# A new written-out order for an attention and feed-forward kernel on one core

## The chip, the cores and the metric

The kernel runs on one core of one Trainium2 chip. The metric is the device time of one execution in microseconds; the time of a version is the median of its runs. A core has five engines that the text names as the profile does: PE (TensorE, matrix products; PEld is its loading of weights), DVE (VectorE), ACT (ScalarE), POOL (GpSimd) and SP (SyncE, which here only issues transfers). Each engine works through its own list of instructions in order and waits on semaphores for the others.

## The reference

Inputs are q, k and v of shape (8, 8, 576, 64) (batch, heads, sequence, head width) and two weight matrices, all float32.

```python
def _attn_ref(q, k, v):                       # factor = 4
    q_d = q.reshape(B, H, Sd, factor, D).mean(axis=3)      # also k_d, v_d
    out_d = sm_attn(q_d, k_d, v_d)                         # attention on 144 pooled rows
    out_up = np.repeat(out_d, factor, axis=2)
    mask = np.abs(pos[:, None] - pos[None, :]) < factor    # a band of 7
    scores = np.where(mask, scale * np.matmul(q, k.transpose(0, 1, 3, 2)), -1e9)
    out_local = np.matmul(softmax(scores), v)
    return out_up + out_local

def _moe_ref(x, w_in, w_out):                 # x: (4608, 512), d_ff = 2048
    h = x @ w_in
    return (h - np.tanh(h)) @ w_out
```

The sum of the two attentions, laid out as 4608 tokens by 512, goes through the feed-forward part; its result is the output.

## The kernel before

The work is cut in two ways. Attention runs over 32 pairs of heads (8 batches of 4 pairs); the feed-forward part runs over 8 blocks, one for each batch, and block b needs all four pairs of batch b. The attention of later pairs is spread between the matrix products of earlier blocks.

**One pair** passes through these steps. SP loads k and q (tile `st`, line 341, 256 KB each), v (tile `vst`, line 365, two halves of 160 KB), and the last 64 rows of k and q of a batch (tile `sr`, line 353; for the first batch these two loads are issued by ACT). Casts to bf16 make `qr` (line 499), `rr` (line 489) and `vw` (line 425). For the first eight pairs PE turns `qr` over by identity matmuls (line 506; `rr` at line 529 into `rT`), and ACT or DVE copy the result to `kt` and `kq` (lines 511, 516, 533, 561, 566); for the later pairs SP issues a transposing transfer instead (line 550, line 544). Pooled q and k go to `qkd` (line 613 to 621 on PE for the first four pairs, lines 587 to 602 after). PE then makes the scores (lines 650, 660, 666), ACT the exponentials in three pieces into `E` (lines 671, 675, 679), DVE or POOL multiply by the band mask (line 706), PE sums pooled v for the first twelve pairs (line 456, from `vw`) and multiplies E with v (line 720). The result is divided (lines 736, 738), turned back by PE (line 763) or by SP (line 775), and joined into `xT` (line 756).

**One block** is 16 products with w_in (line 797, four matmuls of 128x512 each, issued as two halves), tanh on ACT into `u` (line 809), a subtraction on DVE into `gT` (line 812), and the product with w_out. The 64 left tokens of two batches share steps of their own (lines 824, 835, 837, 850). The first block multiplies with w_out plainly (line 878); the other seven do it in seven half-size products (line 1018) of sums and differences: `token_sums` (line 953) forms sums of quarters of gT, called S0 to S3, each choosing DVE or POOL, and `weight_sums` (line 927) those of w_out. ACT and POOL gather the results in `y`, and SP stores them (line 908).

**The order** is written out by hand. Each of 2,199 operations is recorded in a `Plan` together with what it reads and writes. Then `emit` goes through a string `TURNS`, in which two characters (base 62, digits, capitals, small letters) number one operation, and emits the operations in exactly that sequence. Thus the sequence fixes the order on each of the engines, SP's transfers among them, while the semaphores still hold back what isn't ready. Four more strings belong to it: `ENGINES` has a letter for each of the operations that may run on more than one engine (D for DVE, A for ACT, P for POOL); `BANKS` picks the PSUM banks; `FILL` puts matmuls on zeros ("filler", line 1227) ahead of an operation, a bank and a count behind its number; `BEHIND` lists pairs of operations of which the first waits for the second, for engines that share a port.

The operations that the next parts speak of are these. Number `10` is the cast of `rr` of batch 0, `11` and `12` are the casts of k and q of pair 0, `01` is a one-element copy on ACT (line 1150, tile `gate2`), recorded with a price of 1650 ns. `13` and `17` turn k and q of pair 0 over on PE. `3d` is the first matmul of the first block. `7V` is the issue of the second half of v of pair 11, `Ai` that of the transposing transfer of pair 13, `A9` the cast of v of pair 11, `BA` the sum of pooled v of pair 11 on PE (line 456). `Yb` is S0 of the last block.

SP has eight transfer semaphores: an issue waits until the transfer eight issues before it has landed.

Of the kernel before, what the change touches and what calls it, by code (L numbers as in the profile page):

```python
# [101 lines left out]
def kernel(  # L102
# [49 lines left out]
    ]  # L152

    TURNS = (
        "000E0F0I0J06020B0M0N030K0L0G0H0401050O0P0Q0R0D0A0W0X0U0V0e0f101d1e11131B0g0h1512141f1g16"
        "171H1P0Y0Z180C0S0T1I1J1Q0k0l1C1A1L1K19220c0d1M1D1R1S091N1T1u231w0i0j1U2R1O1V240a0b252T26"
        "2G2H1v1j1k08291x1y2Z1l1m27200y1W0o0p071z1E2S1n1o2y2a280m0n1F2U211X1G2b1Y2c2X1Z2V1p1q2d39"
        "0z2I2J2z2W1r5H2n2o1a2Y1s2p2q0q0r3A1b2A2g1c1h1i0s0t3B2B3N3O2e2C3D33303P3Q3C2O1t2t2u3E312P"
        "2D2M2N0u0v3F3G352v2E2f5I2w363H325J343I5L3J37385P5K2K2L5M2h5N2Q5S5O2i2j5U665Q3K5R2F682k5E"
        "3L5v3M2l5T632m5x5V3d5F5X3j643k5y3p5w3q3r5B3s5C613e5D5z3t3v3w5W3l603m3f623u3g3T3U655Y3n3x"  # L160
        "3h0w0x3o6e3y6g3i412r2s426U43475Z3z6c4D3R3S5a444849456T674E6b46694F4G5g5h6B4A406d5b4B4J4K"
        "5c3V3W4P5d4H4L4M4C4Q3X3Y4R5k5l4N6V4I6X5e5f6W4S4V6Y4b5m5n6Z6f4O4T4c4d6a4e2x4h4U7A4i4j4f4W"
        "6A4X4Y4g5s4Z4k4n4o4l4a4t4u5G4v5t4z4w3Z3a4m6C6h6j556i506D4p6E4x514q526Q4r4y7D536F4s567B7F"
        "576G586H7f3b3c6R8854597C7g895A728d7E5u6k7I71967G6l976m7H6y8e6z8E8j8F8k737J76779C7K6n7L7l"
        "74757m6o7M8K7N8p7O6I6J9D6p6u6v8qCG5i5j8L787rCB6K6L798v6M6N9f8w5o5p7s9g8x8Q5q5r9Z7xCD6w6x"
        "8R6s6tCF9h8S9i6q6r7yCC9j7X6O6PCE9I9k9J9a9m7b9l9b9c7z7cCH7Y7d7h9t9u9T6S7i7e9U7P7Q9O9V7Z9W"
        "9v9w9P7j9XAB7n7R7S7a9Q7oAA7k9Y9n70ACAD7t7p9oAd9p9d809zA09e81AG7q9qAbAcA79rA1A2827uAeAH9s"
        "847T7UA8857v83AgAI86Ah7w8AAKBDAiAj878BAJ8GCI8H8C8MATAUAEAF8I8NBaBb8V8DAMAm7V7W8W8J8OAo9x"
        "9y8Z8XALBGBH8fAq8a8PAnAN8Y8bBF8gAkAOApBEAP8l8hBMBIBJ8mAt8c8r8n8s8iA98yB0B1Ar8o8z8tEHEIDx"
        "BA908u92DtAVAW93BNBB91B2B3Al98ELEMCJ9EENEO9F94BOA5A6AsBP99BQBcBd959KBiEJEK9A9LEaAu9G9BDy"  # L170
        "BqBKBr9MDzE0E3AvCLAwBRBsBLCM9HE48T8UCRAZAaBtBTEb9NByBjE5E6CKCSE7EcEdBzEAC0BSC1BgBhE8AQCY"
        "C6BUCZE1C7C8CoARCpC9CABVEgE2BWCuA3A4CvB8B9ASAxF8D0EiEPEQAyBXEhAzEkAXAYD2BYEuEvD3BZDuCXIF"
        "D8EwExF7EjBkBlD9FeElDvF9FABmEeCaDEE9CbAfCgFTFUEmChEfIeIfEVBnCnFhFiEBCmBuBoBvEWEXEYDGFDBw"
        "IcIdDHECBCFEDMEDIgIhC2EnFfDNBxC3F2FFBpC4FGF3CNDSIGFBCOFgFHC5CTIJFjFkCUCPCcFnCdFIFoCVB4B5"
        "DTCQDUDFCeB6B7DZFKBeBfCfDaJxG3G4EoFCDfFVFWCiFZCWCjEEEFIKCqEpCkEqCrD1FlCwETEUCsCxClFpDwFJ"
        "FqD4ILIMCyD5IPFsDiD6CtIQDjF4F5DoFmCzErEsIHDpD7DAFrDBMUDqG1G2DIFaFRFSDCDJFtDOFXFYDKDPDDJS"
        "9R9SDVDQDLEGFbFcDWDbEyEzDRDXDcG7G8IwDkDYDdF0F1DlMVG9GJDeDmGOJREZGTDnERESGUFuGHFLIkIlINFv"
        "DrDsGZGIHhIIGcGhIOGaGiGnGbGuGsFMIvGzFNFdH0GAH5EtFwFOFPFxHmHAHrF6IRJ1FyFzHCITJ2HDISGtHIG5"
        "G6HNIVIxIyHwIqHSJ3IUHUK0K1J4FQHVHaG0J5JTJUIWJ7J6GDIuGEIXIrIiIjIYHfGFHTGKGBGCIzGLGGJEJFJ8"
        "GMJzJGJHHgGPJ0IZIaJXGQGNGVJ9GWJAGRJYImInGdJVGeMrMsGSJyGXJZIoIpHBGfGjGYK2K3GkJaHxGoK6GpGg"  # L180
        "GlMxMyI0GqGmGvIsItMZJWGwJMH1K7H2JOJPJbJNI5JmJnH3GrMYIAJkJlJdIBH4MWH6GxICH7IbK4K8GyH8HEMa"
        "MbKAHJMeK9HKHOJcJBJCHLHFH9HPMfHGJeHMMvMwJsHQHWJKJLHHKCHXNADgDhHbJfHYJtHRHcMtMuKRK5HiJgJI"
        "JJHjKBJuJvHnHZHdHoMzN0HkMgHeKJKKHsHpHlKLKMI1MhJqJrKuI2HtMcKDI3HqNBM4MiNGM5NCNDHuI4MAMkI6"
        "NHHvI7JhJiKZI8KSKaKEOCKFMdKwHyHzKbJDI9KcJQKxL2NEKvKGKHKhJwKiNFL3MjIDIEKjL9KkMlLAKpLPMmKq"
        "KrQmLQMnKsKtNhLVLWNTNUN5MBN6LbNIKILdNKNgLeNJJjNiNjLjLkNMNLKVO1O2LpKWNmN7N8NNL8NnKTKULrKX"
        "NOLqLBKPKQNPNkLCKNKONlLHKYODLIMGNoOELsOLNpOHOILxLOLyLNKdJoJpNqKeOMMoMpKlKfNbMJNrNsKmNVNW"
        "MKM3KnNcONOFOGQnKgMPO7OPKyOOKoQqNzO0KzMQLcNQNRL0L4MXL5L1LDN3N4L6OQLENdNeLJMRLFO8OaObLKMq"
        "ORL7NtN1N2LROJLGLSN9QrNuLXNvLTQwRJRKLfOSLLLUNwNxLYOKNSLMLgLlOTQsQtOULZLmQxLtLhLuLaRSOVOW"
        "LnQyOgLvLzLoM0RTNfRDRELiM6NyOeOfR0M7LwM1RBRCMCMDM8M2O3O4QoMLMEM9O9OAMMOqOXOYOZMFMNOvRURV"
        "QuP0MOQzP1OoOkOiOjP6OlNZNaOrQvOhOsNXNYR1P9RFRGOpOwOmSJSKOxOtPER9RAOnR2RYPFRlRmPKOuOyO5O6"  # L190
        "P2PPRWP3RHRIP7R3P4RnRoOzV1PARXV2PBP5RNPGR4PHRZR5PCPLPIPSS4PDR6R7PMPTPJPNRaRORPRQPUPYRzRb"
        "PdPVRtPZPORyPeRcPaPRP8S0S1PWPfS5PlRePbPmSURpRqPXOBPgV3RLRMS6PnPqOcOdSWS7PvPoSNSOPrRdRrRs"
        "PwPsMSMTQ3RuPxQ4PtR8PcQ5PyQ8PhQ9Q6SPQFQAV5RfSRSSSAQBQGSVQKS2RgSQSZSaQLQHSdQPQMQIQQRvRwRx"
        "PjRhPiSXSYPkS3PpQNQYV6SLSMPuQRSeQES8PQQZPzSfQaQ1QSQ0V7V8ShQ2QpQ7QbQCVUSjRiRjQJSgS9QOQTSH"
        "SISbRRSBQDVBMHMIQdV9QUSqSrT6VAVCSCTTSDQeScQXSiSESFQcQhTRQfQiT7TUVTT8SyQjTZSzTaVZQgVDT9VE"
        "VVVWVOTETSUbVFTFVHSsStUcTgQkQlTGTHThSkTMVGTwV4TPTQTxSlVPSmTNTOU2VaU3VQVRUhRkU8VIVXSnSoUA"
        "VJVYVuUBVKUGUHTfVvVbUMTiSGVfTjVoVcUOVpToUPVdSpVqVrSTTpVwTvT2T0T1VxT3SuSvVeUiVySwSxUUT4Vz"
        "UVVLVMTuVgT5UNVsTAW0UaTBTIVmVhViTJVnTVTKU9TWUnVjVkW1TXTLUqTCW9UoUpUrVtTbQVQWTDTcWAW2TkW3"
        "TdTlW7UwTYTmWBVNTnUxWDTqWCTeVSW4W5TyUyTrWFW8U4WETsTzUCTtVlU0WGU1U5UDW6WHWIUIUEUJU6UQUFWJ"
        "WKURUKU7UWUXULUzV0USUdUYUTUeUjUfUZWLUsUkUgUtWSUuWXUlWcUvWMUmWTWUWQWYWNWZWRWeWaWfWOWmWsWV"  # L200
        "WPWdWxWWWiX4WbWgX5WtWhWkWyXAWzWnWuWlX0XFWoXGWjWpXNWqX6XOXSX7XXWvXPWrWwXHXBXIXYXCXfXZXTXD"
        "XkXaXgXlXQXrXhXwY1X1XiX3XUX8XqXVY2X2XxX9XEXvXJXsXyYAYBXmXzXLXMXnXRXWY0XbYOY3YFXcXdXtY4Y5"
        "XKXeY6YPXjXuXoYbYCY9YGYdYHXpYEYJYDY7Y8YQYKYIYRYSYLYTYUYcYMYNYVYeYWYfYiYgYZYaZ2YXYYYjYkYw"
        "YxZ3YyZ4YhYzYlZ0YmYnZ5Z1YoYpZ7YqZ6YrZAZ8Z9YvYsZBYtYuZCZDZJZEZKZHZFZGZOZIZPZQZRZSZLZMZN"
    )
    ENGINES = (
        "DDDDADDAAPPDAAPADADADDDDPDDDDDADPDAPDPDDAADPADAAAPADAAADDDDDDAPAADAAPPPDDDPPADAAAPPPPDAA"
        "PPADADPPPPDDPPPPAAPPPPDAAAADPPDADDAADDDDAPPPDDPPDADAPPAAPPDDAAPPPAAPPDDPPADDDDDPPDAPPAAP"
        "PDPDDAPPAAPPDPPPADPAADPDDPPADPPAADDDDPPDDDDDPPPAPPAADPDPDPAPPAADDDPDDAPPAAPPDDPPAPPPAAPD"
        "PDPPADDDDDPPPAPPAADPDPDDAPPAAPPDPDPADPAADDDPPPAPPPAADDDPPDDDDDDPPPAPPAAPPDPPPAPPDAPPDDPD"  # L210
        "APPAAPDDDPPAPPPDAPDDDDPADDDDDPPPAPPAAPPDPDPPDPAAPPDPPPDPAAPPDPPPPPDPDPPPDADDDDD"
    )
    BANKS = (
        "0123456017206457012760113005223301301030203210230101210031212003321100112311002032011320"
        "3101102201310203110023210201301001012110130100113200123101231023110021010131032110321321"
        "0301120310120031021101001002101021130203110032103213120130120310120120012010112030110210"
        "1010030210301230102310230123674512365714327601524736120"
    )
    FILL = (
        "13715 1771 1L61 1w31 2431 1E01 1X72 3351 3H21 2h72"  # L220
    )
    BEHIND = (
        "1B11 2S0y 5H0z 2f3F 655W 7A6a AmAF AnAL BiAs EgCZ DFFo JSFt IvGb IrJ6 MYJN MfJc NBKu QmL"
        "A LqNn NcNr O8OQ RYOp V1P7 SUS5 R8Ru Q0PQ VPVG VuRk VpVo UNVz VlWE"
    )

    const = ctx.enter_context(tc.tile_pool(name="const", bufs=1))
# [60 lines left out]
    V, A, T, GP = nc.vector, nc.scalar, nc.tensor, nc.gpsimd  # L288
# [970 lines left out]
```

## Time and profile before

| | us |
|---|---|
| median of 3 runs | 316.26 |
| the runs | 314.4, 316.26, 320.43 |
| the profiled execution | 313.24 |
| its span, first to last instruction | 311.5 |

The profiled execution took 313.24 us, of which 311.5 us are its span. In the profile a window's line gives for each engine the busy time inside it with the number of instructions in brackets; a row of the timeline gives start, duration, engine, line, operation, tiles and shape, and in square brackets the idle time ahead of it with what ended it. A row of the timeline merges equal instructions that follow each other (x12). Matmuls are pipelined, so the duration of a merged row is a little longer than the time after which the next instruction can start; the chain of waits has that time itself.

### The profile page before, as it was taken

What the parts mean: (1) busy time and instruction counts of PE and PEld (TensorE: products, weight loads), DVE (VectorE), ACT (ScalarE), POOL (GpSimd) and SP (SyncE); (2) the same over time, 40 slices, a digit from 0 to 9 for tenths busy, and PEclk for the clock granted to TensorE, in tenths of its full rate; (3) what the DMA queues carried; (4) which work ended last, traced back from release to release, by engine and by line L of the source; (5) the groups of instructions that cost most, each with busy time, mean ns of one, the idle gap of its engine ahead of it and who ended that gap; (6) DMA issues with size and microseconds to landing.
All of it is one profiled execution on the core that took longest, in us unless ns stands there. A gap on an engine that the chain in (4) does not pass through costs nothing.

```text
span 311.5 us, 7779 instructions
## 1 busy us (share of the span) xinstructions
PE 299.8 (96%) x2982; PEld 198.2 (64%) x2982; DVE 248.4 (80%) x443; ACT 213.4 (68%) x378; POOL 167.4 (54%) x222
## 2 busy tenths in 40 slices
PE   6898999999899999999999999999999999999994
PEld 2575555554477655875587755656878655468783
DVE  3888875689988988998998978977995888564944
ACT  2888883289778887889886788888947675554110
POOL 5198869046684368338771379387624582911200
PEclk9999999999999999999999999999999999999999
DMA  6999999599998999989999999999999653000224
GB/s 208 266 269 239 219 240 186 137 258 260 222 227 238 281 182 257 258 154 233 262 288 262 242 230 177 242 260 252 150 184 196 151 171 93 3 0 2 100 71 136
DMA packets 120870, 60.81 MB, mean 195 GB/s; under 512 B 88832, under 2 KB 118528, under 8 KB 120832
## 3 DMA queue, kind: packets, MB, share of 16 engines
q1 hardware_dynamic: 115968, 55.53, 78.8%
q0 software_dynamic: 4224, 4.19, 8.1%
q10 hardware_dynamic: 640, 0.59, 0.6%
q8 instruction: 23, 0.38, 0.5%
q14 instruction: 15, 0.12, 0.1%
HBM read 44.04 MB, written 9.44 MB: 172 GB/s over the span
## 4 chain that ended last, share of the span: by engine, by line
PE 83%; DMA 7%; POOL 5%; SPq 1%; issue 1%; DVE 0%; ACTq 0%; POOLq 0%; DVEq 0%
PE ps L797 32%; PE ps L1018 28%; PE ps L720 5%; PE ps L850 4%; PE ps L878 4%; PE ps L824 4%; PE ps L650 2%; DMA vst<-in_v_dram 2%; DMA st<-in_q_dram 2%; DMA sr<-in_q_dram 2%; DMA kq<-qr 1%; POOL qr L499 1%; PE ps L666 1%; PE ps L763 1%; POOL qkd L592 1%
## 5 line engine op out<-in xcount | busy, mean ns | idle before, releaser
L797 PE MATMUL ps<-xT,w_in_sb 128*128 128x512 bf16 x512 | 121.4, 379 | 0.0
L812 DVE TENSOR_TENSOR gT<-ps,u 128x512 bf16<-128x512 f32 x128 | 84.9, 686 | 21.6 <-ACT u L809 21.0
L809 ACT ACTIVATE u<-ps 128x512 f32<-128x512 f32 x128 | 74.2, 599 | 29.8 <-PE ps L797 25.0
L797 PEld LDWEIGHTS <-w_in_sb 128*128 128x128 bf16 x512 | 47.7, 98 | 47.9
L1018 PEld LDWEIGHTS <-gT 128*128 128x128 bf16 x672 | 64.1, 98 | 15.6
L1018 PE MATMUL ps<-w_out_sb,gT 128*128 128x256 bf16 x336 | 43.4, 273 | 0.0
L1018 PE MATMUL ps<-Tw,gT 128*128 128x256 bf16 x336 | 42.3, 273 | 0.0
L499 POOL CAST qr<-st 128x512 bf16<-128x512 f32 x49 | 29.8, 616 | 16.4 <-DVE vw L1156 6.1
L671 ACT ACTIVATE E<-ps 128x912 bf16<-128x912 f32 x32 | 29.7, 930 | 9.1 <-PE ps L660 6.7
L738 DVE TENSOR_TENSOR ln<-ps,r 128x768 bf16<-128x768 f32 x32 | 30.6, 957 | 1.2 <-DVE r L736 0.2
L1089 POOL TENSOR_TENSOR y<-y,keep 128x512 f32<-128x512 f32 x12 | 15.2, 1273 | 26.1 <-ACT y L1039 15.0
L577 ACT COPY kt<-kq 128x576 bf16<-128x576 bf16 x23 | 27.2, 1187 | 1.7 <-DMA kq<-qr 1.5
L587 POOL TENSOR_TENSOR half<-kq 128x576 f32<-128x576 bf16 x16 | 20.4, 1276 | 13.4 <-ACT kq L572 5.5
L720 PEld LDWEIGHTS <-E 128*128 128x128 bf16 x576 | 21.4, 97 | 6.2 <-POOL E L706 1.5
L592 POOL TENSOR_TENSOR qkd<-half 128x288 bf16<-128x288 f32 x20 | 16.5, 823 | 13.0 <-DVE r L736 5.8
L679 ACT ACTIVATE E<-ps 128x576 bf16<-128x576 f32 x32 | 21.0, 655 | 1.8 <-PE ps L666 1.8
L706 DVE TENSOR_TENSOR E<-E,mask 128x1152 bf16<-128x1152 bf16 x26 | 20.2, 785 | 1.4 <-ACT E L671 0.7
L837 DVE TENSOR_TENSOR gL<-ps,u 128x512 bf16<-128x512 f32 x16 | 15.9, 1020 | 5.2 <-ACT u L835 5.2
L756 POOL TENSOR_TENSOR xT<-lT 128x336 bf16<-128x336 bf16 (+1 forms) x26 | 17.0, 678 | 5.2 <-DMA lT<-ln 3.1
L720 PE MATMUL ps<-vw,E 128*128 128x65 bf16 x320 | 19.0, 193 | 0.7 <-POOL E L706 0.7
L1039 ACT COPY y<-ps 128x512 f32<-128x512 f32 x19 | 11.1, 587 | 11.9 <-PE ps L1018 11.6
L425 ACT CAST vw<-vst 128x640 bf16<-128x640 f32 x24 | 17.6, 731 | 1.1 <-DMA vst<-in_v_dram 1.1
(122 smaller groups left out, 470.5 us busy)
## 6 DMA issues: line engine op xcount, KB each, us to landing
vst<-in_v_dram SPq DMA_DIRECT2D x64, 160.0 KB, 4.4
st<-in_k_dram SPq DMA_DIRECT2D x32, 256.0 KB, 4.4
st<-in_q_dram SPq DMA_DIRECT2D x32, 256.0 KB, 4.5
out_dram<-y SPq DMA_DIRECT2D x14, 512.0 KB, 3.3
v<-in_v_dram SPq DMA_DIRECT2D x20, 256.0 KB, 4.5
w_in_sb<-in_moe_w_in_dram POOLq DMA_DIRECT2D x4, 512.0 KB, 10.7
w_out_sb<-in_moe_w_out_dram POOLq DMA_DIRECT2D x4, 512.0 KB, 7.9
vr<-in_v_dram SPq DMA_DIRECT2D x8, 128.0 KB
```

Of the source, the lines that this page charges most:

```text
L499: (eng, ns, lambda dst=dst, src=src, fn=fn: fn(out=dst, in_=src), port)
L577: ("ACT", 1180, lambda: A.copy(out=ktv, in_=src), False),
L587: eng.tensor_tensor(out=half, in0=flat[:, 0:576], in1=flat[:, 576:1152], op=ALU.add)
L671: A.activation(out=E[s][:, :, E0:E0 + 456], in_=at(s1)[:, :, PS0:512], func=AF.Exp, scale=SCALE)
L679: A.activation(out=E[s][:, :, EP:EW].rearrange("p h (i c) -> p h i c", i=2)[:, :, :, 0:G], in_=at(s2)[:, :, 120:408].rearrange("p h (i c) ...
L706: eng.tensor_tensor(out=el, in0=el, in1=mask.unsqueeze(1).to_broadcast([128, 2, S]), op=ALU.mult)
L720: T.matmul(po[:, hh, 65 * n:65 * n + 65], E[s][:, hh, e:e + 128], vv, start=start, stop=stop)
L738: op("DVE", 960, lambda: V.tensor_tensor(out=ln[s].rearrange("p n (h d) -> p h n d", d=D), in0=blocks()[:, :, :, 0:64], in1=r[s].unsqueeze ...
L797: T.matmul(at(name)[:, 0, :], w_in_sb[:, dc, fc * 128:(fc + 1) * 128], xT[dc][:, c0:c0 + S].rearrange("p (c g) -> p c g", c=4)[:, :, 0:128 ...
L809: op("ACT", 600, lambda: A.activation(out=u[us], in_=at(name)[:, 0, :], func=AF.Tanh), reads=[("hd", kb, fc)], writes=[("u", us)], uses=[n ...
L812: op("DVE", 690, lambda: V.tensor_tensor(out=gT[g][:, fc, :], in0=at(name)[:, 0, :], in1=u[us], op=ALU.subtract), reads=[("hd", kb, fc), ( ...
L1018: T.matmul(dst, left[:, f, 128 * j:128 * j + 128], right[:, f, :], start=(first and e == 0 and f == 0 and (j == 0 or apart)), stop=(e == 1 ...
```

## The change

The five strings are replaced by five others; no operation is added, removed or resized. In the new strings 95 of the operations that may choose run on another engine: the counts by engine go from 413 to 417 on DVE, 381 to 388 on ACT and 196 to 185 on POOL, and stay at 705 on PE and 246 on SP. There are 26 fillers in both. The number of `BEHIND` pairs grows from 31 to 37. All lines behind the strings move by one (line 797 becomes 798).

The first line and the strings that are short, in whole:

```diff
     TURNS = (
-        "000E0F0I0J06020B0M0N030K0L0G0H0401050O0P0Q0R0D0A0W0X0U0V0e0f101d1e11131B0g0h1512141f1g16"
+        "00020G0H0A0I0J0E0F0C0K0L0Y0Z030M0N04050Q0R0O0P1f1g0W0X100e0f12111d1e01130a0b1714151P0g0h"
...
     FILL = (
-        "13715 1771 1L61 1w31 2431 1E01 1X72 3351 3H21 2h72"
+        "13716 1R42 2472 2V62 2b61 2A22 5S51"
     )
     BEHIND = (
-        "1B11 2S0y 5H0z 2f3F 655W 7A6a AmAF AnAL BiAs EgCZ DFFo JSFt IvGb IrJ6 MYJN MfJc NBKu QmL"
-        "A LqNn NcNr O8OQ RYOp V1P7 SUS5 R8Ru Q0PQ VPVG VuRk VpVo UNVz VlWE"
+        "1H1A 2R1C 0y2S 2z21 5Q1G 5P3F 5B5W 635D 6A6d 7172 9U9l AAAB AmAF AnAL DyCJ EgCZ FfCn DFF"
+        "o MUIP EGFt EtGb HTJ6 IbJc NhKu JjLA LqOD LcOC QrQq RyP7 RNP8 PiPQ VTSe R8Si RkTg VZVG V"
+        "nVz W6WE"
     )
```

The stretch of `TURNS` around `7V`, `A9` and `BA`, and the one around `Yb`:

```diff
-        "9v9w9P7j9XAB7n7R7S7a9Q7oAA7k9Y9n70ACAD7t7p9oAd9p9d809zA09e81AG7q9qAbAcA79rA1A2827uAeAH9s"
-        "847T7UA8857v83AgAI86Ah7w8AAKBDAiAj878BAJ8GCI8H8C8MATAUAEAF8I8NBaBb8V8DAMAm7V7W8W8J8OAo9x"
-        "9y8Z8XALBGBH8fAq8a8PAnAN8Y8bBF8gAkAOApBEAP8l8hBMBIBJ8mAt8c8r8n8s8iA98yB0B1Ar8o8z8tEHEIDx"
-        "BA908u92DtAVAW93BNBB91B2B3Al98ELEMCJ9EENEO9F94BOA5A6AsBP99BQBcBd959KBiEJEK9A9LEaAu9G9BDy"
+        "7U7y9X7e7h7P7Q7z7iCE9Y7nAB7o7j9nAA7p7k7t70ACAD809d9o9p9eAdAG81A1A2A77q9qAe9zA0AH7u829rAT"
+        "AU849sA8BD857v7V7W83AIAh867w8AAgAK8B87AMAiAj8GCI8C8H8MAE8IAF8VAVAWAJ8N8D9x9yAm8WB8B98JAo"
+        "8O8ZBaBbAL8X8aAbAcAq8f8YAnIcIdAN8PB0B18bA98gApBGBHAOAk8cBE8l8h8mBFAPAt8rBMBIBJ8s8n8i8y8t"
+        "8z8oDtIeIfArBADx8u9092B2B393BNBB91BgBhAl98As998T8U9EEHEI94CJBOBP9KBQ9F95Dy9A9LBiDzE0AuBR"
...
-        "YxZ3YyZ4YhYzYlZ0YmYnZ5Z1YoYpZ7YqZ6YrZAZ8Z9YvYsZBYtYuZCZDZJZEZKZHZFZGZOZIZPZQZRZSZLZMZN"
+        "YmYxYyYnYhZ2Z3YzYoZ0Z4Z5Z1YpZ6YqYrZ7Z8Z9ZAYsYvZBYtYuZCZDZJZEZKZHZFZGZOZIZPZQZRZSZLZMZN"
```

In the compiled program ACT's first computing instruction carries the load of the activation table. Before, that instruction is the copy `01`; in the changed program `10` and `12` stand ahead of `01` on ACT, so the table load stands ahead of the cast `10` and behind the wait for the second of the two `sr` transfers. `Yb` runs on POOL instead of DVE.

## The prediction

> **What bounds the kernel now.** I read the page's busy times first, then a table of windows, then the waits of PE.
>
> ```profile
> span 311.5 us, 7779 instructions
> PE 299.8 (96%) x2982; PEld 198.2 (64%) x2982; DVE 248.4 (80%) x443; ACT 213.4 (68%) x378; POOL 167.4 (54%) x222
> ```
>
> A busy PE need not be PE at its peak, so 96% alone proves little. The windows show where the rest lies (start and end, length, then PE, PEld, DVE, ACT, POOL busy with counts, granted clock, share of the transfer engines, GB/s).
>
> ```profile
> 0.00:7.35 7.35, 4.72 (x16) 1.75 (x17) 2.60 (x19) 1.47 (x3) 3.63 (x14) 1.00 0.66 199
> 7.35:26.24 18.89, 16.21 (x272) 12.48 (x273) 15.30 (x37) 16.20 (x36) 11.88 (x16) 1.00 1.15 264
> 26.24:29.39 3.15, 2.61 (x52) 2.02 (x49) 2.68 (x9) 2.21 (x5) 3.07 (x6) 1.00 1.18 244
> 29.39:60.00 30.61, 30.61 (x269) 16.31 (x267) 22.44 (x49) 17.28 (x35) 20.36 (x23) 1.00 1.04 200
> 60.00:90.00 30.00, 28.15 (x286) 16.19 (x285) 26.03 (x45) 25.27 (x45) 17.24 (x23) 1.00 1.15 246
> 90.00:290.00 200.00, 200.00 (x1949) 135.22 (x1948) 167.20 (x271) 147.97 (x253) 111.18 (x143) 1.00 0.85 188
> 290.00:311.50 21.50, 17.50 (x153) 14.28 (x150) 12.17 (x17) 2.96 (x5) 0.00 (x0) 0.99 0.34 111
> ```
>
> From 90 to 290 us PE is never idle, and the products run at pitch:
>
> ```profile
> 119.32 5.18 PE ps L797 x24
> 124.50 1.75 PE ps L1018 x16
> ```
>
> That is 216 ns for a 128x512 matmul and 109 ns for a 128x256 one, in a stretch where the transfer engines are 85% busy. No order of the same operations can gain there. What an order can move is the time until the first block starts (29.39 us, 5.85 of it idle PE), the 1.85 us idle between 60 and 90, and the 4.0 us at the end, of which the last store and the closing of the program are most.
>
> **Part 1, the stalls between 60 and 90.** The largest:
>
> ```profile
> 73.86 2.11 SPq L550 DMA_TRANSPOSE kq<-qr  x1
> 77.14 6.20 DMA vst<-in_v_dram
> 80.02 2.76 PE L797 MATMUL ps<-xT,w_in_sb 128*128 128x512 bf16 x12
> 83.46 0.72 POOL L425 CAST vw<-vst 128x640 bf16<-128x640 f32 x1 [1.86 <-DMA vst<-in_v_dram]
> 84.23 0.45 PE L456 MATMUL ps<-vw,pick 128*128 128x128 bf16 x5 [1.45 <-POOL vw L425]
> ```
>
> The twelve matmuls could hand over at 80.02 + 12 x 0.216 = 82.61; `BA` starts at 84.23, so PE loses 1.6 us. It waits for the cast `A9`, that for the transfer `7V`, issued at 77.14 and in hand 6.2 us later, where the median landing is 4.4:
>
> ```profile
> vst<-in_v_dram SPq DMA_DIRECT2D x64, 160.0 KB, 4.4
> ```
>
> In the old sequence 7V stands behind the transposing transfer Ai, which held SP for 2.11 us, and eleven halves of L797 products (0.43 us each, 4.8 us) lie between 7V and BA, with some 1.0 us of attention matmuls. In the new one 7V stands ahead of Ai, with eighteen halves (7.8 us) and about 1.3 us of attention before BA: 9.1 us of cover against a need of 6.2 + 0.72 and the hand-over, 7.1. So this stall goes even if the landing is as late again. Two smaller ones:
>
> ```profile
> 66.44 0.59 PE L878 MATMUL ps<-w_out_sb,gT 128*128 128x512 bf16 x2
> 67.26 0.45 PE L456 MATMUL ps<-vw,pick 128*128 128x128 bf16 x5 [0.23 <-ACT vw L425]
> PE ps L666 <- POOL qkd L592: 0.2, 1, 0.2
> ```
>
> 67.26 - 66.44 - 2 x 0.216 is 0.4 us, behind another `vst`, and 0.2 behind `qkd`. Together 2.2 us. This is the pattern of the whole change: counting, with the two pitches above, the matmul work that stands between a load's issue and the first use of what it brings, 25 of the 130 loads that are issued after the first block begins have less than 6.0 us in the old sequence and 13 less than 5; in the new one 3 and none. The price of the earlier places is nothing as long as a buffer is free by then; where it isn't, SP waits, and the transposing transfers behind it come late (the slower rival). As new waits I take 0.3 us, between 0 and the 2.2 that went.
>
> **Part 2, the start.** ACT is the engine to follow.
>
> ```profile
> 2.15 1.28 ACT L1150 ACT_TABLE_LOAD   x1 [2.15 <-issue]
> 3.44 0.19 ACT L1150 CAST gate<-lT 1x1 f32<-1x1 bf16 x1
> 6.51 0.43 DVE L489 CAST rr<-sr 128x512 bf16<-128x512 f32 x1 [3.58 <-DMA sr<-in_q_dram]
> 7.35 0.62 ACT L499 CAST qr<-st 128x512 bf16<-128x512 f32 x1 [3.72 <-DMA st<-in_q_dram]
> 25.92 0.32 ACT L566 COPY kq<-rT 128x64 bf16<-128x64 bf16 x1
> 26.43 0.60 PE L650 MATMUL ps<-kq,kt 64*128 64x112 bf16 x16
> 29.39 1.89 PE L797 MATMUL ps<-xT,w_in_sb 128*128 128x512 bf16 x8
> ```
>
> Before, the table load lay in the time in which nothing had landed. Now it stands behind the wait for `sr`, about 6.45, and ends at 7.73; the casts `10` and `12` follow. From there to the copy that frees the scores of pair 5 (at 26.24 before) ACT has 39 instructions where it had 36. By kind the difference is one copy L1150 (0.19), two of L561, two of L621 and one of L511 more, three of L566 fewer:
>
> ```profile
> L566 ACT COPY kq<-rT 128x64 bf16<-128x64 bf16 x6 | 1.8, 303 | 0.0
> L561 ACT COPY kt<-rT 128x64 bf16<-128x64 bf16 x4 | 1.3, 334 | 0.0
> L511 ACT COPY kt<-ps 128x512 bf16<-128x512 bf16 x2 | 1.2, 580 | 0.0
> L621 ACT CAST qkd<-ps 128x288 bf16<-128x288 f32 x1 | 0.4, 396 | 0.0
> ```
>
> 0.19 + 0.67 + 0.79 + 0.58 - 0.91 = 1.3 us, on 16.20 us busy before: 17.5. Without any wait ACT is through at 7.73 + 17.5 = 25.2, 1.0 early; with the 18.89 - 16.20 = 2.7 us of waits that it had before, at 27.9, 1.7 late. One wait is sure: the copy to `rT` needs PE's turning of `rr`, which in the new order follows that of `12`, some 0.5 us. I take the middle, 0.35 late, and leave the 2.96 us from the scores of pair 5 to the first block as they are, since the same kinds of steps (a division, a turning back, a joining) lie there.
>
> The Trainium skill, "ScalarE: Activation LUTs", What ACT_TABLE_LOAD costs, gives 1283 ns for the load and about 1380 ns more for a drain, 2.66 us for a switch. The first figure agrees with the 1.28 here; for the second no row stands here, as the copy starts at 3.44, right behind. By the page the sum would be 1.4 us larger.
>
> Less is also done when the first block starts: two PE steps (pooled v of pair 4, a turning of pair 6) that stood ahead of `3d` now stand behind it.
>
> ```profile
> 39.03 0.45 PE ps L506 x8
> ```
>
> Eight turnings in 0.45 us make 0.22 for a step of four; the five sums of the row at 67.26 take at most 0.45, at the turnings' pitch 0.28: 0.5 us. Part 2 costs 0.35 + 0.5 = 0.85, between -0.5 and 2.2.
>
> **Part 3, the end.** `Yb`, S0 of the last block, moves to POOL, where a form of that size takes 4.07 us against 1.28:
>
> ```profile
> L953 POOL TENSOR_TENSOR gT<-gT 128x2048 bf16<-128x2048 bf16 x1 | 4.1, 4071 | 3.6 <-DVE S L953 3.6
> L953 DVE TENSOR_TENSOR S<-gT 128x2048 bf16<-128x2048 bf16 x7 | 9.0, 1283 | 0.2
> L953 DVE TENSOR_TENSOR gT<-gT 128x2048 bf16<-128x2048 bf16 x13 | 15.9, 1224 | 1.1 <-PE ps L1018 1.1
> L809 ACT ACTIVATE u<-ps 128x512 f32<-128x512 f32 x128 | 74.2, 599 | 29.8 <-PE ps L797 25.0
> L812 DVE TENSOR_TENSOR gT<-ps,u 128x512 bf16<-128x512 f32 x128 | 84.9, 686 | 21.6 <-ACT u L809 21.0
> L1089 POOL TENSOR_TENSOR y<-y,keep 128x512 f32<-128x512 f32 x12 | 15.2, 1273 | 26.1 <-ACT y L1039 15.0
> ```
>
> From the last half of the first product of that block to the first product that reads S2, which follows from S0, 25 PE steps stand, at most 0.44 us each, three of them 0.22 to 0.45: 10.4 us. The chain in that time is tanh and subtraction (0.60 + 0.69), two gathering sums on POOL beside them (2 x 1.27), 4.07 and 1.22 for S2: at most 9.1 us if the sums stand ahead of S0. Over 1 us is left; without cover it would cost the 2.8 us between the two engines. I take nothing.
>
> **The sum.** 313.24 - 2.2 + 0.3 + 0.85 = 312.2 for an execution like the profiled one. The three runs before lie 1.2, 3.0 and 7.2 us above the profiled execution. With fewer loads that can be late I take the middle of the two lower, 2.1: **314.3 us**.
>
> **Rivals.**
> - *The transposing transfers come late* (slower than before). The loads were moved ahead of them, and the one of part 1 held SP for 2.11 us. The chain of waits has such a step:
>
> ```profile
> 65.35 4.62 DMA kq<-qr
> ```
>
> Counted as in part 1, five of the 26 transposing transfers after the first block begins have less than 4.0 us of cover now, four before, and they need 4.6 and a copy. It decides where SP reaches one over 1.5 us later than its place: PE then stands as long as at 82.6, 1.6 us. Two of those are 3.2: 315.4, and with the 3.0 of the median before 318.4. For it: that step stands on the chain. Against: PE stood idle for none of it between 90 and 290 us. 17%.
> - *PE's clock falls at the start.* The fillers, matmuls on zeros, begin the program:
>
> ```profile
> 1.26 4.69 PE L1227 MATMUL ps<-lT 128*128 128x512 bf16 x15 [1.26 <-DVE lT L1149]
> ```
>
> Fifteen at 0.216 would be 3.2 us; the 1.4 more say that some six ran at half pace, a stretch of 2.6 us. Now 16 of them end near 6.2, and then PE has only the turning of `11` until `12` is cast, at about 7.73 + 0.43 + 0.62 = 8.8. If 2.6 us of near-idleness bring half pace back for as long a stretch, 1.3 us are lost: 315.6. Against: the idle 1.4 us ahead of 7.35 left the granted clock at 1.00. 10%. The Trainium skill, "TensorE: Matmul & The Clock Gate", What's actually happening, says that an idle window of some 3.4 us brings the half clock; no run here shows a gap of that length.
> - *The gain isn't there*: the 1.6 us stall was that execution's, or another load takes its place. 314.3 + 2.2 = 316.5. 13%.
> - *The start is quick*: ACT waits little, part 2 gives -0.5, and the runs lie 1.2 above: 313.24 - 1.9 - 0.5 + 1.2 = 312.0. 15%.
>
> The forecast has the remaining 45%, with 312.5 to 316.5 of its own.
>
> **How the numbers follow.** Low end: the quick start without the runs' extra, 310.8. High end: the forecast's execution with the 7.2 us of the highest run before, 319.4. About 2 in 10 stay outside, more of it above. Faster by over 2% would be under 309.9, for which even the quick start must improve: 4%. Slower by over 2%, over 322.6, needs the late transfers twice over: 5%. The rest, 91%, is inside the 2% that a measurement of this kernel can tell from no change.
>
> **What would show it.** The table load on ACT starting near 6.4; the first L798 near 29.7; no wait of PE at L457 near 82; PE full from 90 to 290; the S0 on POOL near 287 with no wait at L1019 after it. Wrong would be: a first L798 after 31.5; PE waiting on `kq` or `kt` at L651; fillers or turnings at 0.43 us after 6 us.

## The result, and the profile after

The changed kernel took 316.71 us in the median of 11 runs (315.4 to 320.45), the kernel before 315.19 us in 11 runs (312.93 to 320.43). The ratio is 1.0061, 95% interval 1.0032 to 1.0091: a small loss where a small gain was forecast. This ratio and those below leave out runs that lie over 1.5% above the fastest of their kernel (here four of before and one of the changed kernel); the medians are of all runs, and their ratio here is 1.0048. The profiled execution of the changed kernel took 317.27 us, of which 315.2 are its span, 3.7 more than the span shown of before.

The page's busy times, and the windows cut at the same times as before (start and end, length, then PE, PEld, DVE, ACT, POOL busy with counts, granted clock, share of the transfer engines, GB/s):

```profile
span 315.2 us, 7772 instructions
PE 301.2 (96%) x2971; PEld 199.4 (63%) x2982; DVE 251.8 (80%) x446; ACT 213.9 (68%) x385; POOL 161.1 (51%) x212
```

```profile
7.35:26.24 18.89, 13.98 (x227) 10.55 (x226) 13.76 (x39) 14.15 (x32) 7.11 (x10) 1.00 1.15 248
26.24:29.39 3.15, 1.74 (x25) 1.70 (x26) 1.00 (x3) 2.41 (x6) 0.09 (x1) 0.66 1.12 336
29.39:60.00 30.61, 29.80 (x306) 17.19 (x308) 25.52 (x51) 20.76 (x44) 22.58 (x26) 0.98 1.08 193
60.00:90.00 30.00, 29.84 (x278) 16.78 (x277) 26.75 (x51) 23.29 (x43) 13.50 (x19) 1.00 1.04 242
90.00:290.00 200.00, 198.33 (x1939) 133.44 (x1940) 168.99 (x275) 148.39 (x256) 107.25 (x138) 1.00 0.87 191
```

Three things differ. PE is busy 13.98 us of the second window instead of 16.21, and the granted clock falls to 0.66 behind it. From 60 to 90 the idle time is nearly gone (29.84 of 30 instead of 28.15). And from 90 to 290, where PE had never been idle, it now has 1.67 us of idle time.

The start, in rows of the timeline; the first two are POOL's issue of the first quarter of w_in (`0q`) and SP's of the q of pair 5 (`2I`), then its cast on ACT, PE's turning of it, and the first block:

```profile
19.57 0.94 POOL L407 DMA_DIRECT2D w_in_sb<-in_moe_w_in_dram  x1
20.05 0.64 SPq L342 DMA_DIRECT2D st<-in_q_dram  x1
...
26.98 0.62 ACT L500 CAST qr<-st 128x512 bf16<-128x512 f32 x1 [2.73 <-DMA st<-in_q_dram]
27.65 0.61 PE L507 MATMUL ps<-ident,qr 128*128 128x128 bf16 x4 [2.69 <-ACT qr L500]
...
33.21 0.38 PE L798 MATMUL ps<-xT,w_in_sb 128*128 128x512 bf16 x1
```

The same steps before:

```profile
19.34 0.47 SPq L341 DMA_DIRECT2D st<-in_q_dram  x1
19.62 1.69 POOL L406 DMA_DIRECT2D w_in_sb<-in_moe_w_in_dram  x2
...
23.19 0.62 ACT L499 CAST qr<-st 128x512 bf16<-128x512 f32 x1 [0.35 <-DMA st<-in_q_dram]
```

`2I` is issued only 0.7 us later than before, but its cast starts 3.8 us later: the transfer took 6.9 us instead of 3.8, and it was issued 0.48 us behind `0q` instead of 0.28 ahead of it. The first block starts at 33.21 instead of 29.39, 3.8 us late. Up to the first L1019 (92.20 instead of 90.45) 2.1 of that come back, and from there to the end another 1.9 are lost. Their place is in the chain of waits (start, length, what):

```profile
162.25 3.95 DMA lT<-ln
...
166.29 0.96 DVE ln L739
167.25 0.95 DVE E L707
168.20 1.15 DVE gT L954
...
169.44 0.70 DVE gT L954
...
170.19 2.36 PE ps L1019 x20
...
174.73 5.52 DMA kq<-qr
```

DVE's division of a pair (line 739) waits for a transposing transfer, and two sums that PE needs stand behind it on DVE: PE loses 0.67 us at 169.5, and 0.95 at 181, behind a `kq`. With 0.34 at 129 (a bank that ACT frees) that is the 1.9. (The rows give 0.50, 0.78 and 0.18 us of idle time for the three, since the merged row ahead of each is drawn some 0.17 us past the matmuls' pitch.)

### The profile page after: what moved, and what is told of

Same layout as the page of the kernel before. It is cut to its first block, busy times and chain, and to the rows that moved or that the text cites. A ratio compares the mean times of both kernels' runs of the same rounds, so it can differ in the third digit from the quotient of the medians.

```text
span 315.2 us, 7772 instructions
## 1 busy us (share of the span) xinstructions
PE 301.2 (96%) x2971; PEld 199.4 (63%) x2982; DVE 251.8 (80%) x446; ACT 213.9 (68%) x385; POOL 161.1 (51%) x212
## 4 chain that ended last, share of the span: by engine, by line
PE 79%; DMA 9%; ACT 3%; DVE 2%; SPq 2%; issue 2%; POOL 1%; ACTq 0%; DVEq 0%; POOLq 0%
PE ps L798 33%; PE ps L1019 23%; PE ps L721 5%; PE ps L879 4%; PE ps L825 3%; PE ps L851 3%; PE ps L651 3%; DMA st<-in_q_dram 2%; DMA kq<-qr 2%; DMA sr<-in_q_dram 2%; DMA vst<-in_v_dram 2%; DMA lT<-ln 1%; PE ps L764 1%; DMA out_dram<-keep 1%; SPq L551 1%
## 5 line engine op out<-in xcount | busy, mean ns | idle before, releaser
L1019 PEld LDWEIGHTS <-gT 128*128 128x128 bf16 x672 | 64.5, 98 | 17.8 <-issue 0.8
L1019 PE MATMUL ps<-w_out_sb,gT 128*128 128x256 bf16 x336 | 43.6, 273 | 0.3 <-ACT keep L1040 0.2
L1019 PE MATMUL ps<-Tw,gT 128*128 128x256 bf16 x336 | 42.3, 273 | 0.5 <-DVE gT L954 0.5
L500 POOL CAST qr<-st 128x512 bf16<-128x512 f32 x45 | 27.2, 619 | 28.8 <-DVE gT L954 11.5
L757 POOL TENSOR_TENSOR xT<-lT 128x336 bf16<-128x336 bf16 (+1 forms) x28 | 18.4, 683 | 17.7 <-DVE gT L954 10.9
L707 DVE TENSOR_TENSOR E<-E,mask 128x1152 bf16<-128x1152 bf16 x28 | 21.9, 786 | 4.2 <-ACT E L676 3.9
L426 ACT CAST vw<-vst 128x640 bf16<-128x640 f32 x23 | 16.6, 734 | 0.3 <-DMA vst<-in_v_dram 0.3
L954 DVE TENSOR_TENSOR gT<-gT 128x2048 bf16<-128x2048 bf16 x13 | 15.9, 1220 | 0.8 <-PE ps L1019 0.6
```

Source lines behind the costliest of these rows:

```text
L500: (eng, ns, lambda dst=dst, src=src, fn=fn: fn(out=dst, in_=src), port)
L707: eng.tensor_tensor(out=el, in0=el, in1=mask.unsqueeze(1).to_broadcast([128, 2, S]), op=ALU.mult)
L1019: T.matmul(dst, left[:, f, 128 * j:128 * j + 128], right[:, f, :], start=(first and e == 0 and f == 0 and (j == 0 or apart)), stop=(e == 1 ...
```

## The experiments

Each ratio is to runs of the kernel before on the same chip. Diffs show stretches of `TURNS` with the pairs set apart. In some expectations `2I` is called the k of pair 5; it is the q.

**Where the loss is made.** Both orders have issued the same operations but one by their 443rd (about 55 us), so the two starts and the two rests can be crossed. `old_start` has operations 0 to 442 of the sequence from the kernel before (order, engines, fillers, pairs) and the rest as changed; `new_start` is the reverse.

> The first 443 operations of the sequence (to about 55 us) in the order, on the engines, with the fillers and pairs of the kernel before; all others as changed. Theory 1, the loss is made in the start (first block at 33.2 us where it was at 29.4, PE's clock at 0.66 in between), and the rest of the changed order is a little better: first block near 29.4, time 1 to 2 us under the kernel before, some 3 us under the changed one. Theory 2, the loss is the late transposing transfers between 150 and 182 us: the time stays near the changed kernel's, 316 to 317. Theory 3, neither half matters alone and the late loads in the profile are chance: within 0.5 us of the kernel before.

> The reverse: the first 443 operations as changed, the rest as before. Theory 1: the first block starts near 33 us again, the clock falls under 1.00 again before it, and the time is the worst of all, 317 to 319 us (the stall of 1.6 us near 82 us comes back as well). Theory 2: the time is that of the kernel before, 315. Theory 3: as the kernel before within 0.5 us.

> The changed kernel once more, for a second profile. Theory 1: the first block starts after 32 us again, with a wait of PE for a cast of q or k ahead of it and a clock under 1.00. Theory 3: the late landing was chance, the first block starts near 30 us in this profile while the median stays where it was, 316.7.

| | old rest | changed rest |
|---|---|---|
| old start | 1 | 1.0043 (0.9993 to 1.0093) |
| changed start | 1.0058 (1.0026 to 1.0090) | 1.0104 (1.0047 to 1.0161) |

`new_start` took 315.01 us, `old_start` 316.19, `changed_again` 315.99 beside 314.37 before, in medians of all runs. By the ratios of the table the two halves add up: the start costs about 0.6%, the rest about 0.4%. The four medians give another split, 1, 1.0058, 1.0020 and 1.0052: the start 0.2% at most, the rest 0.3 to 0.6%. So both halves seem to lose, and which loses more isn't settled.

The first theory fell in one half (the changed rest is no better, though its wait near 82 us is gone) and held in the other: the changed start was late in each profile (33.2, 33.3 and 34.4), with waits for loads between 22 and 28 us, so this was no chance. One thing that it expected of `new_start` didn't come: the wait near 82 us is absent there too (PE is busy 29.79 of the 30 us from 60 to 90), though `7V` stands in its old place.

**The table load.**

```diff
- 10 0e 0f 12 11 1d 1e 01
+ 01 10 0e 0f 12 11 1d 1e
```

> The changed kernel with one operation moved: the one-element copy 01 stands ahead of the cast 10 again, so that the table load (1.28 us) lies ahead of the first landing. Theory 1a, the table load is what makes the start late: the cast 10 starts near 6.45 instead of 7.74, the first block about 1.3 us earlier or more (31 to 32 us), the time 1.3 to 3 us lower. Theory 1b, the start hangs on the order and the landing of the loads (the q of pair 5 issued at 20.05 and in hand at 26.98): the first block still starts at 32 to 33.5 us and the time moves by less than 0.7 us.

The ratio is 1.0005 (0.9964 to 1.0046), 314.59 us. The cast `10` starts at 6.34 instead of 7.55 in `changed_again`, the first block at 32.59 instead of 33.29. So the table load is worth 0.7 us of the first block; the rest of the lateness stays, as theory 1b has it. The time moved as 1a has it: the medians differ by 1.4 us, and the interval of the ratio just misses that of `changed_again` (1.0047 to 1.0161). What the early table load gives beyond the 0.7 us isn't shown; the two profiled executions differ by 0.9.

**The race with w_in.**

```diff
- 0q 0r 31 2d 2p 2q 0z 35 28 1r 3P 3Q 2e 1h 1i 32 1s
+ 31 2d 2p 2q 0z 35 28 1r 3P 3Q 2e 1h 1i 32 1s 0q 0r
```

> The changed kernel with one operation moved: the issue 0q of the first quarter of w_in (512 KB, POOL's queue) stands 10 operations later and waits for ACT's cast of vp of pair 1, so that it starts about 2 us later than the 18.7 us of the second look (near 20.8). Theory A, the loads 0k (v of pair 2) and 2I (k of pair 5), which took 6 to 7 us where their neighbours took 3.2 to 3.8, lay behind that transfer: they land about 3.5 to 4 us after their issue again, PE's waits of 2.5 and 1.0 us near 22 to 27 us go, the clock stays near 1.00, the first block starts near 30 and the time falls by 2 to 3.5 us, to 312.5 to 314. Theory B, the loads are late because SP issues them late or because the transfer engines are full anyway: the waits stay within 1 us and the time within 0.7 us of the changed kernel's 316.0. Against A also: if the first quarter itself comes too late, PE waits at the first L798 for w_in instead and the first block stays at 32 or later.

> The same with the copy 01 ahead of the cast 10 as well (the table load in the time before the first landing). Theory A: another 0.5 to 1 us earlier than w_late, first block near 29.5, time 311.5 to 313.5 and thus under the kernel before (314.4). Theory B: as the kernel with the early table load alone, 314.6.

```diff
- 5H 2n 2o 1a 2Y 1s 2p 2q 0q 0r
+ 0q 5H 2n 2o 1a 2Y 1s 2p 2q 0r
```

> The reverse in the kernel before: 0q moved 3 POOL-free places ahead, in front of the cast 5H on POOL, so that it starts about 1 us earlier, near 18.6. Theory A: loads issued from about 18.5 to 20 (1p, 2I) now take 6 to 7 us, PE waits near 23 to 27 us, the first block starts 2 to 3 us late (31.5 to 32.5) and the time rises by 1.5 to 3 us. Theory B: within 0.7 us of the kernel before.

> The kernel before with 0q (and 0s behind it on POOL) about 0.9 us later, behind ACT's piece of the exponentials at 19.8 to 20.5. Theory A with chance: before, 2I got in just ahead of w_in in the profile (issued at 19.34, w_in at 19.62) and may miss in other runs, which would make its wide spread (311.3 to 318.9); with 0.9 us more the spread narrows, few runs over 316, and the median falls by about 1 us. If w_in itself is needed by then, the first block starts up to 0.9 us later. Theory B: nothing moves beyond 0.7 us.

The second diff is `old_w_early`; in `old_w_late` `0q 0r` stand four operations later than before. `w_late`, `w_late_table` and `old_w_late` also have one more pair in `BEHIND` (`0q1s`, `0q2g`), by which the issue `0q` waits for an operation of ACT. In `w_late`, 0q went out at 21.11 and `2I`, 1.04 us ahead of it, was in hand after 4.2 us. Its rows:

```profile
20.07 0.47 SPq L342 DMA_DIRECT2D st<-in_q_dram  x1
...
21.11 0.94 POOL L407 DMA_DIRECT2D w_in_sb<-in_moe_w_in_dram  x1 [1.82 <-ACT vp L461]
...
24.26 0.62 ACT L500 CAST qr<-st 128x512 bf16<-128x512 f32 x1 [0.18 <-DMA st<-in_q_dram]
...
30.81 0.39 PE L798 MATMUL ps<-xT,w_in_sb 128*128 128x512 bf16 x1 [1.11 <-DMA w_in_sb<-in_moe_w_in_dram]
```

The waits of 2.5 and 0.8 us that `changed_again` has near 25 and 27 us are gone (two of 0.6 to 0.7 are left), the clock stays at 1.00, and the first block comes 2.5 us earlier. The last row has what stands in their place: PE waits for w_in itself. The ratio is 1.0007 (0.9972 to 1.0042) against 1.0104, which was measured on another chip. With the table load early it is 0.9981 (0.9947 to 1.0014), but the first block isn't earlier still: it came at 31.2, behind a wait of 1.6 us for w_in. The reverse, in the kernel before with 0q at 18.97, is the worst of all: 1.0144 (1.0089 to 1.0199) in four runs, first block at 35.0, and PE waits for casts of v:

```profile
PE ps L456 <- POOL vw L425: 5.4, 2, 3.4
```

`old_w_late` gave 1.0014 (0.9974 to 1.0054), no gain; its 0q slipped to 22.38, 2.8 us later instead of 0.9, and the first block came at 32.7, though `2I` was 1.7 us ahead. It tells nothing of the spread.

**A second profile of the kernel before.**

> The kernel before once more, for a second profile of it: the one shown took 313.24 us, 2 us under the median of all its runs on that chip (315.19). If its wide spread is made in the start, the first block starts later than 29.4 us in a run near the median (30 to 32) and the rest, from the first block to the end, takes 282 us again; if it is made behind, the first block is at 29.4 and the rest longer.

It took 317.48 us, well above that chip's median of 314.88, and its start was late too:

```profile
20.19 1.68 POOL L406 DMA_DIRECT2D w_in_sb<-in_moe_w_in_dram  x2
20.77 0.47 SPq L341 DMA_DIRECT2D st<-in_q_dram  x1
...
27.90 0.62 ACT L499 CAST qr<-st 128x512 bf16<-128x512 f32 x1 [4.48 <-DMA st<-in_q_dram]
28.57 0.40 PE L506 MATMUL ps<-ident,qr 128*128 128x128 bf16 x4 [2.90 <-ACT qr L499]
```

Here `2I` went out 0.58 us behind `0q` and took 7.1 us; the first block came at 33.7, and from there to the end it was 282.1 us, as in the profile shown. So the sequence before runs the same race and sometimes wins it. That this makes its spread is an inference from the two executions. Some profiles in one table (times of issue, and from issue to landing, from the trace):

| profile | 0q issued | 2I issued | 2I behind 0q | 2I took | first block |
|---|---|---|---|---|---|
| before, as shown | 19.62 | 19.34 | -0.28 | 3.8 | 29.4 |
| old_start | 20.24 | 20.62 | 0.38 | 4.2 | 30.8 |
| before_again | 20.19 | 20.77 | 0.58 | 7.1 | 33.7 |
| old_7v (below) | 21.08 | 19.81 | -1.27 | 4.5 | 30.8 |
| old_7v_again (below) | 20.04 | 20.73 | 0.69 | 6.4 | 33.9 |
| old_w_early | 18.97 | 20.00 | 1.03 | 9.0 | 35.0 |
| changed | 19.57 | 20.05 | 0.48 | 6.9 | 33.2 |
| changed_again | 18.68 | 19.33 | 0.65 | 6.9 | 33.3 |
| table_early | 18.99 | 19.62 | 0.63 | 6.7 | 32.6 |
| new_start | 18.75 | 19.48 | 0.73 | 8.3 | 34.4 |
| w_late | 21.11 | 20.07 | -1.04 | 4.2 | 30.8 |
| v4_behind (below) | 19.05 | 17.88 | -1.17 | 3.6 | 30.2 |

Up to 0.38 us behind, `2I` takes some 4 us; from 0.48 on, 6.4 to 9.0. The old order lands on either side, the changed one on the wrong side in all four. The eight profiles that aren't in the table agree: `2I` went out 0.8 to 2.6 us ahead of `0q` and took 3.4 to 4.7 us.

**Loads of v out of the way.** Another way to win the race: `1p` and `1n`, v of pair 4, behind `2I`; and the table load early.

```diff
- 1p 1q 1y 1D ... 1n 1o 0y 39 ... 2I 2J 2z
+ 1y 1D ... 0y 39 ... 2I 2J 1p 1q 1n 1o 2z
```

> The changed kernel with the table load early (01 ahead of 10) and the two loads 1p and 1n (v of pair 4, first read 110 operations later) behind 2I on SP instead of 6 and 4 loads ahead of it; w_in stays where it was. Theory A (what is issued within 3 us of w_in's issue lands after it): 0k and 2I are issued 1 to 3 us earlier, near 16 to 18.5, and land ahead of w_in, by 22.5; PE's waits near 22 to 27 us fall under 1 us in all, the first block starts at 29.5 to 31, w_in is in hand by then, the clock stays at 1.00, and the time is 1.5 to 3 us under that with the early table load alone, so 1 to 2.5 us under the kernel before. Theory B (SP's place doesn't matter, the engines are full): the first block stays at 32 to 33.

> The same start (443 operations), with the rest as in the kernel before. If the rest of the changed order is what costs 1 to 1.5 us in the medians (316.2 with the old start against 314.4 before; 316.0 with the new start against 315.0 with the old rest), this is 1 us or more under the one with the changed rest. If the two rests are alike, they agree within 0.5 us.

> The kernel before with the two loads of v of pair 4 (1p and 1n) behind 2I on SP, as in v4_behind; nothing else. Theory, its spread is the race of 2I (k of pair 5) with the first w_in: 2I is issued about 1 us earlier and lands ahead of w_in in every run, the runs draw together (313 to 316 instead of 312.7 to 318 and more), and the median falls by 0.7 to 1.5 us. Rival, the spread comes from elsewhere: median and spread stay as before.

In both profiles `2I` landed after some 3.5 us and the first block came at 30.2 and 30.7, as theory A has it. But the time isn't 1 to 2.5 us under the kernel before: `v4_behind` gave 1.0036 (0.9998 to 1.0074) and `v4_behind_old` 0.9986 (0.9954 to 1.0019). This is a third pair in which the changed rest costs 0.4 to 0.5%; the intervals overlap in each pair, but all three go the same way. In both, PE waited 1.5 us for `qkd` just ahead of the first block, behind a cast on POOL that waited for a load behind w_in. `old_v4`, the edit on the kernel before, gave 0.9979 (0.9945 to 1.0014), 313.28 us, but runs up to 317.67. Its profile was of a run of 316.65, in which the start was quick (29.2) and the wait of part 1 twice as long as before, with the clock falling behind it:

```profile
86.49 0.69 PE L456 MATMUL ps<-vw,pick 128*128 128x128 bf16 x5 [3.25 <-POOL vw L425]
```

```profile
60.00:90.00 30.00, 26.75 (x223) 15.03 (x221) 24.64 (x44) 22.87 (x40) 16.44 (x22) 0.94 1.11 233
```

So the spread of the kernel before seems to have at least two sources, and taking one away doesn't close it.

**Part 1 alone.**

```diff
- 7v 83 Ag AI 86 Ah 7w 8A ... 7V 7W 8W
+ 7v 7V 7W 83 Ag AI 86 Ah 7w 8A ... 8W
```

> The kernel before with the transfer 7V alone (and the marker 7W of its landing) 32 operations earlier, ahead of the transposing transfer Ai, as the changed kernel has it. Theory, part 1 of the prediction: the wait of PE for the v of pair 11 near 82 to 88 us, 1.6 to 2.2 us in three profiles with the old start, goes, nothing takes its place, and the time falls by 1 to 2 us under the kernel before. Rival: Ai and the transfers behind it come later for it, PE waits for kq or kt instead, and the time stays within 0.7 us.

> The kernel before with 7V alone moved, a second time. If its gain is real, the ratio is 0.995 to 0.999 again; the narrow spread (312.4 to 315.0 in 12 runs) isn't expected to come again, since the race of 2I with w_in in the start is the same as before.

> Both edits on the kernel before: 7V ahead of Ai and v of pair 4 behind 2I. If they add up, 2 to 3 us under the kernel before, ratio 0.991 to 0.994, and under old_7v alone (0.997). If old_7v had already had all of it, ratio 0.996 to 0.998.

`old_7v` gave 0.9970 (0.9943 to 0.9997), and on another chip 0.9954 (0.9912 to 0.9997). The wait, found between 82 and 90 us in all five profiles with old start, old rest and `7V` in its old place (1.6 to 3.4 us), is gone in both. Part of the gain is lost again in both, as the rival has it: PE stood idle for 1.24 us at 178.7 behind a `kq`, which was in hand 5.4 us after its issue, and for 0.90 us at 105.3 behind a store of `keep`; in the five profiles with the old place there is no such wait. The narrow spread of the first twelve runs didn't come again. With v of pair 4 behind `2I` besides (`old_v4_7v`) it was 0.9987 (0.9954 to 1.0020): the two edits didn't add up, and why isn't shown (0.95 us of the wait was back in its profile).

**What the changed rest costs.**

```diff
- I9 KT KU NF Kc JD Nz O0 Kh KF ... Kj Kv Mk
+ I9 Kv KT KU NF Kc JD Nz O0 Kh KF ... Kj Mk
```

> v4_behind with one operation moved on DVE: Kv (S2 of a block, 1.2 us) stands ahead of KF (the division of pair 19), which in three profiles waits there 0.2 to 1.5 us for a transposing transfer of SP that comes late, with S2, the next sum and PE's product (a wait of 0.2 to 1.4 us near 167 to 170 us) behind it. Theory, the late transposing transfers are what the changed rest costs: PE's wait near 167 us goes, and against the kernel before the ratio falls from v4_behind's 1.0036 by 0.3 to 0.5 per cent, to that with the old rest (0.9986). Rival, the wait only moves (to kq, kt or y somewhere behind): the ratio stays within 0.2 per cent of 1.0036.

The wait for `gT` near 167 us (1.2 us in `v4_behind`) is absent in `s_first`, and PE's busy time between 90 and 290 us goes from 198.45 to

```profile
90.00:290.00 200.00, 199.61 (x1947) 134.91 (x1945) 169.69 (x277) 147.22 (x253) 108.98 (x136) 1.00 0.85 186
```

That alone isn't the edit's doing, for the second profile of the changed kernel, with the rest unedited, has the same:

```profile
90.00:290.00 200.00, 199.59 (x1956) 134.97 (x1958) 169.64 (x277) 149.26 (x256) 108.12 (x139) 1.00 0.84 190
```

Of the seven profiles with the changed rest as it is, three have no wait of PE over 0.2 us in that window (`changed_again`, `table_early` and `w_late_table`, 199.6 busy) and four do (198.2 to 198.8); in `w_late` it is 1.4 us behind a store of `keep` at 103.5, and not a transposing transfer. So the waits come in some executions and not in others. The ratio is 1.0015 (0.9977 to 1.0053) against 1.0036 on another chip: at the edge between the two answers, and the intervals overlap. The late transposing transfer is shown as a wait; that `s_first` takes it away, or that it is the whole cost of the rest, isn't.

**A version under both.** `new_best` is `v4_behind_old` with `5R` ahead of `5v` on POOL; `new_best2` moves the load `1h` ahead of `1p` besides.

```diff
- 5N 5v 3H 5O 5U 5R 66
+ 5N 5R 5v 3H 5O 5U 66
...
- 2I 2J 1p 1q 1n 1o 2z ... 2e 1h 1i 32
+ 2I 2J 1h 1i 1p 1q 1n 1o 2z ... 2e 32
```

> v4_behind_old (changed start with table load early and v of pair 4 behind 2I, old rest) with the sum 5R (qkd) ahead of the cast 5v on POOL: 5v waits for 2n, which lands behind w_in at 28 us, and PE waited 1.5 us for qkd behind it. The first block starts at 29 to 29.7 instead of 30.2 to 30.7, the time is 0.7 to 1.5 us under v4_behind_old: ratio 0.994 to 0.997. If w_in or something else is needed by then, the first block stays at 30.2 and the ratio at 0.9986.

> new_best with one more load moved on SP: 1h (the last rows of v of batch 1, 128 KB) stands ahead of 1p instead of seven loads later, so that it lands ahead of w_in or soon behind it. In new_best it was issued at 22.05 and landed at 34.38, and PE waited 1.5 us for the sum made of it. Theory (loads behind w_in are late): that wait goes, nothing else moves, the ratio to the kernel before falls from 0.997 to 0.993 to 0.995. Rival: the 0.5 us that its bytes take ahead of the others makes 1p, 1n or 2n late, and the ratio stays at 0.997.

`new_best` gave 0.9970 (0.9936 to 1.0004), 312.81 us, first block at 29.4. Its last wait in the start is one more load behind w_in, in the chain of waits:

```profile
22.05 12.33 DMA vr<-in_v_dram
```

`new_best2` gave 0.9936 (0.9898 to 0.9973), 312.93 us where the kernel before took 315.44: the best of all, 1.2% under the changed kernel by the two ratios. The wait for that load was gone in its profile, which also has the rival's: 1.7 and 1.2 us behind the first matmul of the block, for casts of `1n` and `2n`, now in hand later. The interval reaches the rival's 0.997 and overlaps that of `new_best`, so the last step isn't decided.

## Why the prediction was wrong

- **Part 2, the start, is the step that failed.** It took "the middle, 0.35 late", and 0.85 with the work left over, between -0.5 and 2.2; the first block came 3.8 us late, after the 31.5 that the prediction named as a sign of being wrong. The table load starts at 6.45 as said, and 0.7 us of the first block hang on it. What was missing is the order in which bytes land. The working followed ACT's queue and took the waits of before as the upper end, 2.7 us in all. But the count of cover was made for "the 130 loads that are issued after the first block begins", so the loads of the start weren't in it, and `w_in` on POOL's queue was in no count. `w_late` and `old_w_early` show that this decides most of it: with the place of `0q` alone the first block moves from 33.3 to 30.8 in one order, and in the other to 35.0 from 29.4 or 33.7, the two that its profiles have.
- **The execution that was read had won the race.** Part 2 was added to a start of 29.39 us; the second profile of the kernel before has 33.7. That fits with the profiled pair differing by 4.0 us and the medians by 1.5.
- **Part 1 was right in its mechanism**: the wait near 82 us went (0.3 to 0.5% by itself), the cover of 9.1 us sufficed, and PE's idle time from 60 to 90 fell from 1.85 to 0.16. That it needed the move of `7V` isn't so: with the changed start and `7V` in its old place the wait is absent as well.
- **"As new waits I take 0.3 us" was too low for this execution.** It was 1.9 in the profile, by the mechanism of the first rival (transposing transfers that come late), at one sixth of the chance. That rival looked for the wait on `kq`; here it also came by `lT`, through DVE, where sums stand behind a waiting division. In `changed_again` the same order has almost none of it. Its share of the time isn't settled: the crossed pairs put the rest at 0.4 to 0.5%, and that is with the wait near 82 us already gone.
- **The sum.** From the execution read to the one of the changed kernel it is 3.8 for the first block, less the 2.1 that came back, plus 1.9: 3.7 us of span where the prediction had 1.05 less. The shift from the profiled execution to a typical run, taken as 2.1, was about right for the kernel before (313.24 and a median of 315.19), but the changed kernel's median lies 0.6 under its own profiled execution. It was taken as noise in the order before, where it is in part a race that the new start lost in each of its four profiles. The runs don't say how much of the measured loss each term makes.
- **The clock rival** named the right mechanism at the wrong place: not the 2.6 us after the fillers (1.00 in that window), but the wait at 25 us, behind which the clock fell in each of the four profiles that have the changed start with nothing done about the race.
- **Part 3 was right**: S0 ran on POOL from 292.06 for 4.07 us, and no product waited for it.

## What to carry to other kernels

Where a start is bound by transfers, list every load with issue, landing and first use up to the first full-rate work, over all queues together: here 512 KB on POOL's queue took a load that SP issued half a microsecond behind it from some 4 us to 6.4 or more. A single profile of a kernel whose runs spread shows one side of its races: look at where it stands among the runs, and price a change against both sides. An order's local win (here 1.6 us by a load placed earlier) says nothing about the places where the same order gives something up: cross the halves before believing either, and take more than one profile of each.

## What the runs showed of the hardware

- A load of 512 KB on POOL's queue (the first quarter of w_in) slowed the loads of SP's queue, but didn't stop them. In the second profile of the changed kernel SP's loads landed until 21.7 us and the next at 24.8, 3.1 us later (3.5 and 3.9 in `table_early` and `new_start`); `2I` landed at 26.2, and the quarter of w_in, issued ahead of it, at 28.0. From 19.0 to 20.5 us SP's queue alone moved 1459 packets, 0.37 MB; from 22.0 to 24.5, beside w_in, 269 packets, 0.21 MB, and w_in's queue 297 packets, 0.30 MB. The Trainium skill, "DMA: Bandwidth & Descriptors", Queues, rings and completion order, says that each transfer engine takes turns between its queues a packet at a time. The nearly equal numbers of packets agree with that; whether the profile counts as a packet what the page does, no run here shows.
- The clock's half-speed stretches inside the program lasted 3.41 or 6.83 us in the traces. They came behind waits of PE of 2.3 to 3.4 us in eight profiles, and of 1.4 to 1.6 us in six (in `old_7v` at 14.7 us, in `w_late_table` at 32.1), while other waits of 1.4 to 1.8 us left the clock at full speed (1.84 us, ended at 8.4, in `before_again`). The Trainium skill, "TensorE: Matmul & The Clock Gate", What's actually happening, puts the fall to half speed after one idle window or more, of some 3.4 us: the lengths of these stretches fit that window, but each of the waits ahead of them was shorter than it, so the trace agrees with its length and not with its condition.
